# A Fourier-mixing kernel on one core: channel mixing added straight from PSUM, a fourth y buffer, and another order of waiting work

## The chip, the cores and the metric

One Trainium2 chip, one of its cores. Five engines run their own instruction streams in order and meet through semaphores: TensorE (PE, with its weight loads shown as PEld), VectorE (DVE), ScalarE (ACT), GpSimd (POOL) and SyncE (SP), which here issues every DMA. The metric is the device time of one execution in microseconds.

## The reference

Eight batches of 3136 tokens with 256 channels. A global filter in the frequency domain (along the tokens), then a mixing block: real part of a two-dimensional FFT, a residual, a layer norm and two dense layers.

```python
X = np.fft.rfft(x, axis=1)
Y = X * (filt_r + 1j * filt_i)[None, :, :]
x = np.fft.irfft(Y, n=x.shape[1], axis=1)

mixed = np.real(np.fft.fft(np.fft.fft(x, axis=1), axis=2))
u = x + mixed
un = (u - mean(u)) / np.sqrt(var(u) + 1e-06)
out = u + np.maximum(un @ w_ch1, 0.0) @ w_ch2
```

w_ch1 is 256 by 1024, w_ch2 1024 by 256.

## The kernel before

All FFTs are matrix products on PE, with float32 operands split into two float16 parts (a high part, cast by ACT, and the remainder, subtracted by DVE or POOL); three products hh, hl, lh give the accuracy. The FFT of 3136 = 112 x 28 is done in two stages each way, with a DMA through DRAM between the stages to turn the layout.

Per batch b these steps run as generators that the main loop advances a step at a time:

- forward1: seven loads x (L319), a maximum over each for scaling (mx, absmax, L257), then 14 times: cast and subtract (x16), three matmuls into bank s1 (L343), copy and remainder (ast), and a store to d1 (L347).
- forward2: seven loads at from d1 (L367); spectrum: matmuls into bank s2 (L388, L389), product with the filter on DVE and POOL (yt, t2), split and transpose by DMA into z (L414); fold: sums eo, which the channel mixing reads later; inverse1: matmuls (L450 to L452), split into bt, store to d2 (L456).
- inverse2: seven loads b2 from d2 (L484), 14 times matmuls into bank y (L502), scaling by ACT into ys (L509), and stores to dy in DRAM (L488). dy is the filtered x.

The second part works on groups of 256 frequency slots, that is two tiles t of 128, each with both tokens k of a slot (which share the mixed spectrum); there are 49 groups. fetch(g) loads y from dy (L558) into one of three buffers. prepare(g) does the channel mixing on PE into a PSUM bank pm (mix, L571), lets ACT copy it scaled to m (L619), lets POOL form sums and differences sd of the two halves (both, L581 and L582), lets DVE add them to y (add, L588 and L589), computes the layer norm's statistics (st, mv, sb: L639 to L656), the normalized un on DVE (L663), its split u16 (ACT L668, then POOL L670), and transposes it by DMA into ut (L671). Then come eight pairs of products per group: first_product into bank h (L693), ReLU by ACT (L702) and remainder by DVE (L703); second_product into acc (L722), two pairs later; after the eighth, DVE adds acc to y (L731) and y is stored (L734). A product below is one of these 392 pairs.

PSUM has eight banks: four named psf, which s1, s2, i1, y, mix and some small ones share in turn, two for h, two for acc.

The order has two makers. The main loop (L893) emits products and, between them, steps of the FFT stages of coming batches, paced by constants (RISE, EARLY, SOON, LOAD_AT and so on). A scheduler then lays out each engine's instructions in an order of its own, in which ready work can pass work that waits; after(key) forbids that: what is emitted under it stands behind the marked instruction. On the chip every engine, SP's DMA queue too, takes its list strictly in order.

Of the kernel before, what the change touches and what calls it, by code (L numbers as in the profile page):

```python
# [35 lines left out]
STEPS = 22 + 7 * 5  # L36
BACK = 14
EARLY = 0.4
RISE = 30
SOON = 860  # L40
LOAD_AT = (15, 16, 17, 18, 19, 25, 26, 23)
LOAD_AFTER = (6, 7, 8, 9, 10, None, None, None)
LOAD_IN = ("ys", "ys", "ys", "ut", "ut", "ys", "ys", "ys")
WIDEN_AT = (22, 22, 26, 50, 51, 52, 53, 53)
BOUND_AT = (60, 73)
SPLIT_AT = (60, 98)
# [143 lines left out]
def _program(ctx, tc, nc, a, NB):  # L190
# [33 lines left out]
    ones = cp.tile([1, 128], F32, name="ones")  # L224
    eo = cp.tile([128, 2, 2, RING], F16, name="eo")
# [7 lines left out]
    nc.vector.memset(ones, 1.0)  # L233
    nc.scalar.activation(beta[:1], ones[:, 0:1], AF.Sqrt)
# [121 lines left out]
    def forward2(b, d1, d2):  # L356
        al = cp.tile([128, 2], F32, name=f"alpha_{b}")
        nc.vector.tensor_tensor(al[:, 0:1], sxs[b][:, 0:1], pF[:, 0:1], op=ALU.mult)
        nc.vector.tensor_scalar(al[:, 1:2], al[:, 0:1], 1.0 / 64, None, op0=ALU.mult)
# [17 lines left out]
        def spectrum(ch, hf):  # L377
# [5 lines left out]
            p = bank(f"s2_{b}_{ch}_{hf}")[:, :448].rearrange("p (r n) -> p r n", r=2)  # L383
            for u in range(8):
# [3 lines left out]
                nc.tensor.matmul(o, w, s2[:, U, 0].rearrange("p (r k) -> p r k", r=2), start=True, stop=False)  # L388
# [72 lines left out]
        far = 2 if b else 3  # L461
        for c in range(far):
            load(c)
        for c in range(9):
# [9 lines left out]
    def inverse2(b, d2):  # L474
# [6 lines left out]
        def load(c):  # L481
            if c < 7:
                bts[c] = fp.tile([112, 4, 2, 256], F16, tag="b2", name=f"b2_{b}_{c}", bufs=2)
                nc.sync.dma_start(bts[c].rearrange("p j h c -> p (j h) c"), d2v[:, 8 * c : 8 * c + 8])  # L484

        def store(k, s, r, ys, c, j0):
            rows = dy[k, 224 * c : 224 * c + 224].rearrange("(j s q) c -> s q j c", j=4, s=2)
            nc.sync.dma_start(rows[s, :, j0], ys[r : r + 28, j0])  # L488

        load(0)  # L490
        for c in range(14):
# [7 lines left out]
            for js, t in parts:  # L499
                for i in range(2):  # L500
                    for h in range(2):
                        nc.tensor.matmul(  # L502
                            p[64 * h : 64 * h + 64, js],
                            i2[:, t, h, i],
                            bt[:, o + js.start : o + js.stop, h],
                            start=i == 0,
                            stop=i == 1,
                        )
            nc.scalar.activation(ys[:, o : o + 2], p, AF.Copy, scale=al[:, 1:2])  # L509
# [69 lines left out]
    def both(sd, m):  # L579

        nc.gpsimd.tensor_tensor(sd[..., 0, :], m[..., 1:128], m[..., 129:], op=ALU.add)  # L581
        nc.gpsimd.tensor_tensor(sd[..., 1, :], m[..., 1:128], m[..., 129:], op=ALU.subtract)  # L582

    def add(o, mm, parts):

        for h in range(2):
            c = slice(128 * h + 1, 128 * h + 128)
            nc.vector.tensor_tensor(o[..., c], o[..., c], parts[h], op=ALU.add)  # L588
# [375 lines left out]
```

## Time and profile before

| | us |
|---|---|
| median of 3 runs | 1606.58 (1602.94 to 1613.36) |
| profiled execution | 1607.78, span 1605.9 |
| granted TensorE clock, mean | 0.946 |
| DMA moved | 273 MB, mean 170 GB/s |
| ACT, POOL instructions | 1302, 803 |

The profile shows one execution. The page's first part gives an engine's busy time and its share of the span; a window row the same for a stretch of it, with the granted clock and the share of the time in which the 16 DMA engines were busy. A waits row says which instruction stood idle for whom, in total, how often and how long at most. A group row has the instructions of one line and shape: count, busy time, mean of one, and the idle time of their engine just ahead of them. A timeline row has its start, its length, and in brackets the idle time before it with what ended that.

The start has its own character: in the first 160 us the clock granted to TensorE was 0.66 on average, and products began at 159.

### The profile page before, as it was taken

What the parts mean: (1) busy time and instruction counts of PE and PEld (TensorE: products, weight loads), DVE (VectorE), ACT (ScalarE), POOL (GpSimd) and SP (SyncE); (2) the same over time, 40 slices, a digit from 0 to 9 for tenths busy, and PEclk for the clock granted to TensorE, in tenths of its full rate; (3) what the DMA queues carried; (4) which work ended last, traced back from release to release, by engine and by line L of the source; (5) the groups of instructions that cost most, each with busy time, mean ns of one, the idle gap of its engine ahead of it and who ended that gap; (6) DMA issues with size and microseconds to landing.
All of it is one profiled execution on the core that took longest, in us unless ns stands there. A gap on an engine that the chain in (4) does not pass through costs nothing. (4 is left out here: it accounts for less than half of the span.)

```text
span 1605.9 us, 30431 instructions
## 1 busy us (share of the span) xinstructions
PE 1414.0 (88%) x11217; PEld 943.0 (59%) x11217; DVE 1142.5 (71%) x2557; ACT 706.2 (44%) x1302; POOL 634.4 (40%) x803
## 2 busy tenths in 40 slices
PE   4344989898989989898988999899998999999998
PEld 1332666566665656555665666556675666666666
DVE  7784978697676668686667877767877779655552
ACT  4454634363435444363433643345543645433331
POOL 4463058216722176114751165311861057421110
PEclk9555999999999999999999999999999999999999
DMA  7999558867875786756875786855987488634430
GB/s 232 262 204 246 132 139 179 207 173 178 183 193 146 185 178 152 214 152 156 195 176 157 196 176 153 206 152 158 208 187 189 133 208 195 160 100 125 114 78 27
DMA packets 446261, 273.14 MB, mean 170 GB/s; under 512 B 235392, under 2 KB 412592, under 8 KB 446112
## 3 DMA queue, kind: packets, MB, share of 16 engines
q1 hardware_dynamic: 446112, 271.20, 68.6%
q8 instruction: 88, 1.44, 0.4%
q14 instruction: 61, 0.50, 0.1%
HBM read 113.31 MB, written 102.76 MB: 135 GB/s over the span
## 5 line engine op out<-in xcount | busy, mean ns | idle before, releaser
L693 PE MATMUL h<-ut,w1s 128*128 128x512 f16 x2352 | 593.6, 387 | 40.9 <-DVE h L703 37.9
L722 PE MATMUL acc<-w2s,h 128*128 128x256 f16 x4704 | 595.8, 275 | 17.3 <-DVE y L731 15.6
L722 PEld LDWEIGHTS <-h 128*128 128x128 f16 x4704 | 458.8, 99 | 151.3 <-issue 30.1
L703 DVE SCALAR_TENSOR_TENSOR h<-h,h 128x512 f16<-128x512 f32 x392 | 266.9, 683 | 215.2 <-ACT h L702 214.6
L702 ACT ACTIVATE h<-h 128x512 f16<-128x512 f32 x392 | 232.4, 596 | 386.7 <-PE h L693 378.2
L693 PEld LDWEIGHTS <-w1s 128*128 128x128 f16 x2352 | 224.5, 99 | 273.2 <-issue 82.8
L670 POOL TENSOR_TENSOR u<-un,u 128x512 f16<-128x512 f32 x94 | 110.9, 1194 | 370.9 <-ACT u L668 276.2
L581 POOL TENSOR_TENSOR sd<-m 128x254 f32<-128x254 f32 (+1 forms) x64 | 41.9, 655 | 317.8 <-ACT m L619 278.6
L401 POOL TENSOR_TENSOR yt<-yt,t 128x224 f32<-128x224 f32 x105 | 70.4, 671 | 151.7 <-DVE t L397 90.8
L588 DVE TENSOR_TENSOR y<-y,sd 128x254 f32<-128x254 f32 (+1 forms) x224 | 104.7, 511 | 23.3 <-DMA y<-dy 22.8
L409 POOL TENSOR_TENSOR y<-yt,y 128x448 f16<-128x448 f32 x105 | 110.7, 1058 | 14.0 <-ACT y L405 13.7
L343 PE MATMUL s<-x,s 112*112 112x512 f16 x336 | 100.7, 403 | 7.5 <-DVE x L338 5.4
L509 ACT ACTIVATE ys<-y,alpha 128x512 f32<-128x512 f32 x112 | 76.4, 688 | 66.1 <-PE y L502 56.1
L405 ACT CAST y<-yt 128x448 f16<-128x448 f32 x112 | 62.9, 564 | 85.6 <-POOL yt L402 83.8
L388 PE MATMUL s<-s,at 112*128 112x56 f16 x896 | 67.1, 194 | 35.6 <-DMA at<-d 27.0
L257 DVE TENSOR_REDUCE mx<-x 112x1 f32<-112x1024 f32 x56 | 67.8, 1213 | 40.5 <-DMA x<-x 40.4
L502 PE MATMUL y<-b,i 112*64 112x512 f16 (+1 forms) x480 | 76.8, 403 | 21.6 <-DMA b<-d 21.2
L455 DVE TENSOR_TENSOR bt<-i,bt 112x512 f16<-112x512 f32 x112 | 75.2, 680 | 26.1 <-ACT bt L454 26.0
L393 DVE TENSOR_TENSOR yt<-s,ft 128x448 f32<-128x448 f32 x112 | 68.2, 613 | 35.5 <-PE s L389 34.8
L454 ACT CAST bt<-i 112x512 f16<-112x512 f32 x112 | 64.9, 582 | 62.8 <-PE i L452 39.8
L345 ACT CAST ast<-s 112x512 f16<-112x512 f32 x112 | 65.2, 583 | 61.4 <-PE s L343 52.2
L338 DVE SCALAR_TENSOR_TENSOR x<-x,sx,x 112x512 f16<-112x512 f32 x111 | 89.2, 808 | 2.8 <-ACT x L337 2.3
(130 smaller groups left out, 1826.7 us busy)
## 6 DMA issues: line engine op xcount, KB each, us to landing
x<-x SPq DMA_DIRECT2D x56, 448.0 KB
d<-ast SPq DMA_DIRECT2D x112, 224.0 KB
at<-d SPq DMA_DIRECT2D x56, 448.0 KB
d<-bt SPq DMA_DIRECT2D x112, 224.0 KB
b<-d SPq DMA_DIRECT2D x56, 448.0 KB
out<-y SPq DMA_DIRECT2D x98, 256.0 KB
y<-dy SPq DMA_DIRECT2D x92, 256.0 KB
dy<-ys SPq DMA_DIRECT2D x208, 112.0 KB
```

The costliest lines, as they stand in the source:

```text
L338: nc.vector.scalar_tensor_tensor(x16[:, 1], x, sx[:112, 1:2], x16[:, 0], op0=ALU.mult, op1=ALU.subtract)
L343: marks["pe", q] = nc.tensor.matmul(p, s1[:, hs], x16[:, hx], start=i == 0, stop=i == 2).ins
L409: last = half(b, hf == 1).tensor_tensor(y16[:, :, 1, :112], ytv, y16[:, :, 0, :112], op=ALU.subtract)
L455: nc.vector.tensor_tensor(bt[:, :, 1], p, bt[:, :, 0], op=ALU.subtract)
L502: nc.tensor.matmul(p[64 * h : 64 * h + 64, js], i2[:, t, h, i], bt[:, o + js.start : o + js.stop, h], start=i == 0, stop=i == 1,)
L509: nc.scalar.activation(ys[:, o : o + 2], p, AF.Copy, scale=al[:, 1:2])
L588: nc.vector.tensor_tensor(o[..., c], o[..., c], parts[h], op=ALU.add)
L670: marks["u16", g] = low.tensor_tensor(u16[:m, :, :, 1], unv, u16[:m, :, :, 0], op=ALU.subtract).ins
L693: nc.tensor.matmul(p[:, c0 : c0 + n].rearrange("p (t k q) -> p t k q", k=2, q=m), w1s[:, d, hw, 128 * f : 128 * f + 128], utv[:, ts, :, d, ...
L702: nc.scalar.activation(h[:, 0, :nt], p[:, :nt], AF.Relu)
L703: nc.vector.scalar_tensor_tensor(h[:, 1, :nt], p[:, :nt], 0.0, h[:, 0, :nt], op0=ALU.max, op1=ALU.subtract)
L722: nc.tensor.matmul(acc[:m, k], h[:, hh, c0 : c0 + m], w2s[:, f, hw], start=f == 0 and k == 0 and i == 0, stop=f == 7 and k == 1 and i == 2,)
```

## The change

- DVE now adds the mixed channels to y straight from the PSUM bank pm, scaled by alpha or its negative in the same instruction: per tile one addition over 4 x 127 elements, two over 2 x 127, one over the four end channels. The copies m and the sums sd, with their tiles, are gone; a single row's Nyquist part is added by itself (add_nyquist).
- un is computed by ACT (scale and bias) instead of DVE; the steps for sb are written as fewer fused operations, and EPS is ACT's bias.
- y has four buffers instead of three. fetch(g + 2) is called two products earlier, and its load stands behind the output of the group four back.
- The maxima over x run two loads behind their loads and stand behind an h of the products; the adds to y stand behind an h; the first s2 matmul and the first y matmul of a batch stand behind a first product; loads of b2 stand behind the latest store to dy.
- forward2 keeps three loads at ahead for every batch, takes two empty steps (PAUSE) after them, and inverse2 one; the pacing constants are set anew. Of these numbers the diff shows only some.

```diff
-BACK = 14
-EARLY = 0.4
-RISE = 30
-SOON = 860
+PAUSE = 2
+BACK = 15
+EARLY = 0.5
+RISE = 28
+SOON = 930
...
     def forward1(b, d1):
...
-        for q in range(7):
+        lag = 2 if b else 0
+        for q in range(7 + lag):
             with after(("y", 0), ("un", 0)) if b == 1 else nullcontext():
-                nc.sync.dma_start(xs[q], a["x"][b, :, 4 * q : 4 * q + 4])
-                absmax(m[:, q : q + 1], xs[q], AX.XY)
-            yield
+                if q < 7:
+                    nc.sync.dma_start(xs[q], a["x"][b, :, 4 * q : 4 * q + 4])
+                if q >= lag:
+                    with after("h"):
+                        absmax(m[:, q - lag : q - lag + 1], xs[q - lag], AX.XY)
+            if q < 7:
+                yield
...
+            order = after("pe") if b and ch == 0 else nullcontext()
...
+                with order if u == 0 else nullcontext():
+                    nc.tensor.matmul(o, w, s2[:, U, 0].rearrange("p (r k) -> p r k", r=2), start=True, stop=False)
...
-        far = 2 if b else 3
+        far = 3
         for c in range(far):
             load(c)
+        for _ in range(PAUSE):
+            yield
...
-                nc.sync.dma_start(bts[c].rearrange("p j h c -> p (j h) c"), d2v[:, 8 * c : 8 * c + 8])
+                with after("dy"):
+                    nc.sync.dma_start(bts[c].rearrange("p j h c -> p (j h) c"), d2v[:, 8 * c : 8 * c + 8])
...
-        y = ys_of[g] = mp.tile([128, 2, 2, 256], F32, tag="y", name=f"y_{g}", bufs=3)
+        y = ys_of[g] = mp.tile([128, 2, 2, 256], F32, tag="y", name=f"y_{g}", bufs=4)
...
-                with after(("ut", 0)) if g == 2 else nullcontext():
+                with after(("ut", 0)) if g == 2 else after(("out", g - 4)):
...
+    def scaled_add(out, p, al, y):
+
+        nc.vector.scalar_tensor_tensor(out, p, al, y, op0=ALU.mult, op1=ALU.add)
+
+    def add(o, pm, al):
+
+        n = o.shape[0]
+        oh = o.rearrange("p k (h c) -> p (k h) c", h=2)
+        even = pm[:, 1:128].unsqueeze(1).to_broadcast([n, 4, 127])
+        odd = pm[:, 129:].unsqueeze(1).to_broadcast([n, 2, 127])
+        ends = pm[:, 0:129:128].unsqueeze(1).to_broadcast([n, 2, 2])
+        scaled_add(oh[..., 1:], even, al[:, 0:1], oh[..., 1:])
+        for hs, sign in ((slice(0, 4, 3), 0), (slice(1, 3), 1)):
+            scaled_add(oh[:, hs, 1:], odd, al[:, sign : sign + 1], oh[:, hs, 1:])
+        scaled_add(o[..., 0:129:128], ends, al[:, 0:1], o[..., 0:129:128])
...
-        for ps, ts, al in runs:
-            nc.scalar.activation(m[ps, ts], pm[ps, ts], AF.Copy, scale=al)
-            both(sd[ps, ts], m[ps, ts])
-        yield
-        for k in range(2):
-            for ps, ts, al in runs:
-                with after(("u16", 0)) if g == 1 else nullcontext():
-                    add(y[ps, ts, k], m[ps, ts], (sd[ps, ts, k], sd[ps, ts, 1 - k]))
...
+        for t, (g0, g1) in enumerate(tiles):
+            ps = slice(0, g1 - g0)
+            with after(("u16", 0)) if g == 1 else after("h"):
+                add(y[ps, t], pm[ps, t], alpha_of(g0, g1, f"al_{g}_{t}")[ps])
...
-            nc.vector.tensor_scalar(v, v, EPS, None, op0=ALU.add)
-            nc.scalar.activation(r, v, AF.Sqrt)
+            nc.scalar.activation(sb[:m, ks, 0], mv[:m, ks, 1], AF.Sqrt, bias=eps[:m])
...
-                marks["un", g] = nc.vector.tensor_scalar(
-                    un[:m, k], y[:m, t, k], mv[:m, i, 0:1], sb[:m, i, 2:3], op0=ALU.subtract, op1=ALU.mult
-                ).ins
+                nc.scalar.activation(un[:m, k], y[:m, t, k], AF.Identity, bias=sb[:m, i, 1:2], scale=sb[:m, i, 3:4])
...
-        if f == 2 and g + 2 < ng:
+        if f == 0 and g + 2 < ng:
             bring(groups[g + 2][-1][1] - 1)
             fetch(g + 2)
```

How the built program's instructions stand in three places. In the names the first number is the batch or the group, the next the step; h16_9_5 is h of group 9, fifth pair counted from 0. First DVE, where the maxima of batch 3 (mx_3) meet the products of group 9. Before:

```order
L703 SCALAR_TENSOR_TENSOR h16_9_4_5390<-h_9_4_5383,h16_9_4_5390 128x512
L257 TENSOR_REDUCE mx_3_5557<-x_3_0_5550 112x1
L455 TENSOR_TENSOR bt_2_5_1_5423<-i1_2_5_1_5416,bt_2_5_1_5423 112x2x256
L257 TENSOR_REDUCE mx_3_5557<-x_3_1_5551 112x1
L703 SCALAR_TENSOR_TENSOR h16_9_5_5434<-h_9_5_5427,h16_9_5_5434 128x512
L589 TENSOR_TENSOR y_11_5340<-y_11_5340,m_11_5394 128x2x2 x2
L257 TENSOR_REDUCE mx_3_5557<-x_3_2_5552 112x1
L588 TENSOR_TENSOR y_11_5340<-y_11_5340,sd_11_5395 128x2x127 x4
L257 TENSOR_REDUCE mx_3_5557<-x_3_3_5553 112x1
L455 TENSOR_TENSOR bt_2_6_0_5464<-i1_2_6_0_5457,bt_2_6_0_5464 112x2x256
L257 TENSOR_REDUCE mx_3_5557<-x_3_4_5554 112x1
L703 SCALAR_TENSOR_TENSOR h16_9_6_5475<-h_9_6_5468,h16_9_6_5475 128x512
```

The same engine and place after:

```order
L715 SCALAR_TENSOR_TENSOR h16_9_3_5373<-h_9_3_5366,h16_9_3_5373 128x512
L260 TENSOR_REDUCE mx_3_5364<-x_3_0_5357 112x1
L715 SCALAR_TENSOR_TENSOR h16_9_4_5398<-h_9_4_5391,h16_9_4_5398 128x512
L260 TENSOR_REDUCE mx_3_5364<-x_3_1_5358 112x1
L715 SCALAR_TENSOR_TENSOR h16_9_5_5444<-h_9_5_5437,h16_9_5_5444 128x512
L260 TENSOR_REDUCE mx_3_5364<-x_3_2_5359 112x1
L715 SCALAR_TENSOR_TENSOR h16_9_6_5476<-h_9_6_5469,h16_9_6_5476 128x512
L597 SCALAR_TENSOR_TENSOR y_11_5274<-mix_11_5401,alpha_1_1858,y_11_5274 128x4x127
L260 TENSOR_REDUCE mx_3_5364<-x_3_3_5360 112x1
L597 SCALAR_TENSOR_TENSOR y_11_5274<-mix_11_5401,alpha_1_1858,y_11_5274 128x2x127 x2
L597 SCALAR_TENSOR_TENSOR y_11_5274<-mix_11_5401,alpha_1_1858,y_11_5274 128x4
L597 SCALAR_TENSOR_TENSOR y_11_5274<-mix_11_5401,alpha_1_1858,y_11_5274 128x4x127
```

Between two h there stood up to three maxima, and in these rows now one. Second SP's queue shortly before, where the loads of y_11 and x_3 and the output of group 8 stand. Before:

```order
L734 DMA out<-y_8_4077 128x2x256 x2
L671 DMA_TRANSPOSE ut_10_5189<-u16_10_0_5300 128x8x128
L456 DMA d2_2_3099<-bt_2_4_0_5325 112x1024
L558 DMA y_11_5340<-dy_1_3057 128x2x256
L456 DMA d2_2_3099<-bt_2_4_1_5336 112x1024
L414 DMA_TRANSPOSE z_2_6_5177<-y16_1_103 128x8x128
L558 DMA y_11_5340<-dy_1_3057 128x2x256
L671 DMA_TRANSPOSE ut_10_5189<-u16_10_1_5356 128x8x128
L319 DMA x_3_0_5550<-x 112x1024
```

The same queue and place after:

```order
L324 DMA x_3_4_5361<-x 112x1024
L467 DMA d2_2_3029<-bt_2_4_1_5175 112x1024
L574 DMA y_11_5274<-dy_1_2981 128x2x256 x2
L324 DMA x_3_5_5362<-x 112x1024
L467 DMA d2_2_3029<-bt_2_5_0_5221 112x1024
L467 DMA d2_2_3029<-bt_2_5_1_5232 112x1024
L467 DMA d2_2_3029<-bt_2_6_0_5270 112x1024
L324 DMA x_3_6_5363<-x 112x1024
L746 DMA out<-y_8_4046 128x2x256 x2
```

The load of y_11 stood behind the output of group 8 and ahead of the loads x_3; now it stands behind the first five of those loads and ahead of that output. Third DVE where group 5 is made ready (its adds to y_5). Before:

```order
L703 SCALAR_TENSOR_TENSOR h16_3_5_3012<-h_3_5_3005,h16_3_5_3012 128x512
L455 TENSOR_TENSOR bt_1_5_0_2990<-i1_1_5_0_2983,bt_1_5_0_2990 112x2x256
L455 TENSOR_TENSOR bt_1_5_1_3001<-i1_1_5_1_2994,bt_1_5_1_3001 112x2x256
L589 TENSOR_TENSOR y_5_2896<-y_5_2896,m_5_2961 128x2x2 x2
L703 SCALAR_TENSOR_TENSOR h16_3_6_3080<-h_3_6_3073,h16_3_6_3080 128x512
L588 TENSOR_TENSOR y_5_2896<-y_5_2896,sd_5_2962 128x2x127 x4
L639 BN_STATS st_5_3166<-y_5_2896 128x6 x4
```

The same engine and work after:

```order
L715 SCALAR_TENSOR_TENSOR h16_4_7_3524<-h_4_7_3517,h16_4_7_3524 128x512
L597 SCALAR_TENSOR_TENSOR y_5_2820<-mix_5_3007,alpha_0_393,y_5_2820 128x4x127
L245 TENSOR_REDUCE row_x2_3162<-pt_x2_3160 1x1
L597 SCALAR_TENSOR_TENSOR y_5_2820<-mix_5_3007,alpha_0_393,y_5_2820 128x2x127 x2
L597 SCALAR_TENSOR_TENSOR y_5_2820<-mix_5_3007,alpha_0_393,y_5_2820 128x4
L597 SCALAR_TENSOR_TENSOR y_5_2820<-mix_5_3007,alpha_0_393,y_5_2820 128x4x127
```

The adds to y_5 stood behind the sixth and seventh h of group 3, ten products ahead of group 5's first; now they stand behind the last h of group 4.

More of the change, by code (lines that the diff above doesn't have):

```diff
@@ L224, in _program @@
     ones = cp.tile([1, 128], F32, name="ones")
+    eps = cp.tile([128, 1], F32, name="eps")
     eo = cp.tile([128, 2, 2, RING], F16, name="eo")
@@ L356, in forward2 @@
     def forward2(b, d1, d2):
[L357 removed]
+        al = cp.tile([128, 3], F32, name=f"alpha_{b}")
         nc.vector.tensor_tensor(al[:, 0:1], sxs[b][:, 0:1], pF[:, 0:1], op=ALU.mult)
[L359 removed]
+        nc.vector.tensor_scalar(al[:, 1:2], al[:, 0:1], -1.0, None, op0=ALU.mult)
+        nc.vector.tensor_scalar(al[:, 2:3], al[:, 0:1], 1.0 / 64, None, op0=ALU.mult)
         alphas[b] = al
@@ L498, in inverse2 @@
             parts = [(slice(0, 1), 0), (slice(1, 2), 1)] if c == 0 else [(slice(0, 2), 1)]
[L499 to L509, printed above, removed]
+            with after("pe") if c == 0 else nullcontext():
+                for js, t in parts:
+                    for i in range(2):
+                        for h in range(2):
+                            nc.tensor.matmul(
+                                p[64 * h : 64 * h + 64, js],
+                                i2[:, t, h, i],
+                                bt[:, o + js.start : o + js.stop, h],
+                                start=i == 0,
+                                stop=i == 1,
+                            )
+            nc.scalar.activation(ys[:, o : o + 2], p, AF.Copy, scale=al[:, 2:3])
             if o:
@@ L609, in prepare @@
             yield
-        same = len({g0 // NS for g0, _ in tiles} | {(g1 - 1) // NS for _, g1 in tiles}) == 1
-        if same and len(tiles) == 2 and all(g1 - g0 == 128 for g0, g1 in tiles):
-            runs = [(slice(0, 128), slice(0, 2), alphas[tiles[0][0] // NS][:, 0:1])]
-        else:
-            runs = [
-                (slice(0, g1 - g0), slice(t, t + 1), alpha_of(g0, g1, f"al_{g}_{t}")[: g1 - g0])
-                for t, (g0, g1) in enumerate(tiles)
-            ]
-        for ps, ts, al in runs:
-            nc.scalar.activation(m[ps, ts], pm[ps, ts], AF.Copy, scale=al)
-            both(sd[ps, ts], m[ps, ts])
-        yield
-        for k in range(2):
-            for ps, ts, al in runs:
-                with after(("u16", 0)) if g == 1 else nullcontext():
-                    add(y[ps, ts, k], m[ps, ts], (sd[ps, ts, k], sd[ps, ts, 1 - k]))
-            if k == 0:
-                for t, s, pn, al in fix:
-                    nc.scalar.activation(m[s, t], pn, AF.Copy, scale=al[s, 0:1])
-                    both(sd[s, t], m[s, t])
+        for t, s, _, _ in fix:
+            keep = mp.tile([128, 2, 256], F32, tag="un", name=f"keep_{g}", bufs=2)[:, 0]
+            nc.scalar.copy(keep[s], y[s, t, 1])
+        for t, (g0, g1) in enumerate(tiles):
+            ps = slice(0, g1 - g0)
+            with after(("u16", 0)) if g == 1 else after("h"):
+                add(y[ps, t], pm[ps, t], alpha_of(g0, g1, f"al_{g}_{t}")[ps])
+        for t, s, pn, al in fix:
+            add_nyquist(y[s, t, 1], pn, al[s], keep[s])
         yield
@@ L775, in widen_weights @@
             if i % 2 == 0:
-                pairs[0] = mp.tile([128, 2, 512], F32, tag="y", name=f"w_{i}", bufs=3)
+                pairs[0] = mp.tile([128, 2, 512], F32, tag="y", name=f"w_{i}", bufs=4)
             w = pairs[0][:, i % 2]
```

63 lines of the change are left out of this document (30 added, 33 removed).

## The prediction

> **What bounds the kernel now.** I read the busy shares first, then four windows of the trace, the waits inside the long one, and last the timeline at single waits. One page line and the windows (columns: stretch, its length, then busy us and count of PE, PEld, DVE, ACT, POOL, then clock, DMA share, GB/s):
> ```profile
> PE 1414.0 (88%) x11217; PEld 943.0 (59%) x11217; DVE 1142.5 (71%) x2557; ACT 706.2 (44%) x1302; POOL 634.4 (40%) x803
> ...
> 0.00:160.00 160.00, 67.94 (x473) 45.27 (x474) 111.61 (x216) 80.12 (x158) 76.85 (x91) 0.66 0.89 236
> 160.00:350.00 190.00, 174.07 (x1338) 114.67 (x1337) 154.90 (x346) 92.78 (x171) 73.91 (x97) 0.95 0.70 170
> 350.00:1410.00 1060.00, 981.50 (x8045) 658.30 (x8044) 773.99 (x1740) 472.87 (x866) 456.66 (x583) 0.98 0.72 175
> 1410.00:1605.90 195.90, 190.51 (x1365) 124.79 (x1363) 101.97 (x258) 60.37 (x108) 26.97 (x32) 1.00 0.36 88
> ```
> TensorE bounds the kernel from 160 us on, and the change removes none of its matmuls. So all that can be won is its idle time: 92 us in the first stretch, 16, 78.5 and 5 in the others. The first 160 us belong to the DMA queues (share 0.89). The 78.5 us are told by the waits of PE in that window (us, times, longest):
> ```profile
> PE h L693 <- DVE h L703: 32.0, 30, 2.7
> PE s L388 <- DMA at<-d: 16.1, 13, 3.4
> PE acc L722 <- DVE y L731: 11.3, 15, 2.6
> PE y L502 <- DMA b<-d: 9.0, 4, 4.6
> PE i L450 <- DVE mx L257: 2.5, 1, 2.5
> ```
> Two rows of DVE make 43.3 us, two rows of loads 25.1. Why DVE is late shows in its timeline, below with the PE rows that follow from it:
> ```profile
> 458.57 0.68 DVE L703 SCALAR_TENSOR_TENSOR h<-h,h 128x512 f16<-128x512 f32 x1
> 466.15 1.22 DVE L257 TENSOR_REDUCE mx<-x 112x1 f32<-112x1024 f32 x1 [6.90 <-DMA x<-x]
> 467.29 0.68 DVE L455 TENSOR_TENSOR bt<-i,bt 112x512 f16<-112x512 f32 x1
> 467.88 1.21 DVE L257 TENSOR_REDUCE mx<-x 112x1 f32<-112x1024 f32 x1
> 469.01 0.68 DVE L703 SCALAR_TENSOR_TENSOR h<-h,h 128x512 f16<-128x512 f32 x1
> ...
> 469.74 2.64 PE L693 MATMUL h<-ut,w1s 128*128 128x512 f16 x6 [2.67 <-DVE h L703]
> 476.19 1.46 PE L693 MATMUL h<-ut,w1s 128*128 128x512 f16 x6 [1.56 <-DVE h L703]
> ```
> DVE takes its instructions in order. A maximum over x stood ahead of the products' h and waited 6.90 us for x; PE then stood 2.67, 1.56 and more while DVE worked off what had piled up. The other two causes are adds to y that wait for y, and runs of un ahead of the sums that free an accumulator. DVE's own waits for transfers in the same window, then such a run and the PE wait behind it:
> ```profile
> DVE y L589 <- DMA y<-dy: 38.9, 17, 4.8
> DVE mx L257 <- DMA x<-x: 25.5, 9, 6.9
> DVE y L588 <- DMA y<-dy: 8.9, 2, 6.2
> ...
> 577.32 2.46 DVE L663 TENSOR_SCALAR un<-y,mv,sb 128x256 f32<-128x256 f32 x4
> 579.70 0.74 DVE L731 SCALAR_TENSOR_TENSOR y<-acc,beta,y 128x512 f32<-128x512 f32 x1
> ...
> 580.49 1.44 PE L722 MATMUL acc<-w2s,h 128*128 128x256 f16 x6 [2.60 <-DVE y L731]
> ```
>
> **The change part by part.** The group rows that price it (count, then busy us, mean ns of one):
> ```profile
> L588 DVE TENSOR_TENSOR y<-y,sd 128x254 f32<-128x254 f32 x168 | 88.2, 574 | 11.4 <-DMA y<-dy 11.3
> L588 DVE TENSOR_TENSOR y<-y,sd 128x127 f32<-128x127 f32 x56 | 16.5, 322 | 11.9 <-DMA y<-dy 11.5 <-POOL sd L581 0.4
> L589 DVE TENSOR_TENSOR y<-y,m 128x4 f32<-128x4 f32 x84 | 32.1, 418 | 35.6 <-DMA y<-dy 25.8 <-ACT bt L454 4.4 <-ACT h L702 3.5
> L589 DVE TENSOR_TENSOR y<-y,m 128x2 f32<-128x2 f32 x28 | 6.1, 237 | 21.4 <-DMA y<-dy 13.2 <-ACT m L619 8.3
> L731 DVE SCALAR_TENSOR_TENSOR y<-acc,beta,y 128x512 f32<-128x512 f32 x98 | 71.1, 742 | 12.0 <-PE acc L722 12.0
> L393 DVE TENSOR_TENSOR yt<-s,ft 128x448 f32<-128x448 f32 x112 | 68.2, 613 | 35.5 <-PE s L389 34.8 <-POOL ef L422 0.4
> L257 DVE TENSOR_REDUCE mx<-x 112x1 f32<-112x1024 f32 x56 | 67.8, 1213 | 40.5 <-DMA x<-x 40.4
> L663 DVE TENSOR_SCALAR un<-y,mv,sb 128x256 f32<-128x256 f32 x196 | 78.1, 457 | 1.3
> L653 DVE TENSOR_TENSOR sb<-sb 128x4 f32<-128x4 f32 x49 | 13.8, 282 | 1.2
> L619 ACT ACTIVATE m<-mix,alpha 128x512 f32<-128x512 f32 x42 | 28.8, 685 | 13.9 <-PE mix L571 12.9 <-POOL yt L401 0.7 <-DVE y L589 0.4
> L619 ACT ACTIVATE m<-mix,alpha 128x256 f32<-128x256 f32 x8 | 3.7, 473 | 0.9 <-PE mix L571 0.9
> ```
> Added from PSUM: out go DVE's L588 and L589, 88.2 + 16.5 + 32.1 + 6.1 = 142.9 us, ACT's copies (28.8 + 3.7) and POOL's sums and differences. In come four scaled adds for each of 98 tiles, of 508, 254, 254 and 4 elements, one operand in PSUM. The nearest row is L731, the same operation at 512 elements: 742 ns. For smaller ones I take the slope between L393 (448, 613 ns) and L257 (1024, 1213 ns), 1.04 ns an element: 738, 474, 474 and 214, together 1.90 us. Neighbours overlap: of the rows above, the one at 466.15 lasts 1.22 us and the next starts at 467.29, 0.08 before its end, so four less 0.08 each, 1.58 us, is the lower end. That is 155 to 186 us on DVE, 12 to 43 more than goes out. The mean of L588 holds slowed pieces too, so I lean to the upper half, +30.
>
> un moves to ACT: DVE loses 78.1 us; ACT gains 196 times 473 ns (L619 at that size) = 93 and loses its copies of 33. From 706 busy us that makes 766, 48% of the span; the run of un now stands in ACT's queue ahead of the products' h instead of DVE's. Of the small steps for sb six become five: one of 49 times 282 ns less, -14. DVE in all: 1142.5 + 30 - 78 - 14 = 1080, between 1062 and 1093. None of that is on the path by itself, since PE sets the end; it counts where DVE is behind.
>
> Held behind the products: the maxima run two loads behind their transfer and each behind an h already issued; the adds to y stand behind an h as well, and y is fetched two steps earlier into a fourth buffer. Before, a fetch waited for the output of the group three back:
> ```profile
> SPq L558 <- DMA out<-y: 55.2, 25, 5.0
> ```
> With four buffers that output has long landed, so SP no longer stands there, with ut and d queued behind it; a late dy store can still hold a fetch. The order shown above for batch 3 does as the text says: h stand between the maxima, and y 11 is loaded ahead of the output of group 8. So the causes of 43.3 + 2.5 us go. I take three quarters, 34 us: where the maxima, the adds and the x of the next batch meet, DVE still has about as much to do between two h as PE: the wait at 476.19 above came ten us after x had. Ends: a third (15) if that load keeps PE standing, all (46).
>
> Loads (the matmuls of at and of b): the first of each batch is held behind products on PE. Between the last s1 and the first s2 of a batch, and between the last inverse matmul and the first y, the order has about as much product work as before (some 9 us for both), so the transfer itself is no better covered; what helps is the freer SP queue. Of 25.1 us I take 7; ends -5 (the pacing moved against me) and 18.
>
> Start: first products stand behind a PE wait for the maxima of batch 1,
> ```profile
> 159.03 0.34 PE L240 MATMUL pt_x<-ident,mx 112*1 112x112 f32 x1 [12.94 <-DVE mx L322]
> ```
> and in the changed order they come ahead of those maxima. ut's own transposes are issued only shortly before, so of 12.94 I take 5 (0 to 10). What is moved out comes back: batch 1's forward step now starts at product 10 instead of 2, DVE is fuller from there to product 48, and group 5 starts late (the third order place; group 3 is nearly as close): its adds stand behind the last h of group 4, ten products later than before, so that the chain from add to transpose lies between two groups with little else for PE. I estimate some 8 us for it, in a stretch which already lost 16; with the waits that vanish there it cancels, 0 (-10 to +8).
>
> A bank of PSUM is now held until y has come, not until ACT has copied. The order puts the bank's next user one to three products behind the add nearly everywhere, so I cost it at 1 us; if the cover is gone PE waits for the bank in place of h. The other pacing numbers move work by a few products and cost nothing while PE has products to do.
>
> Sum, against the profiled execution (1607.8 us with 1605.9 of span, 1.2 above the median of the runs): 34 + 7 + 5 + 0 - 1 = 45, so 1562.8; against the median 1562.
>
> **The skill against it.** The Trainium skill, "VectorE: DVE Perf Modes", section "Rules for kernel authors", says of elementwise work on a matmul's output to accept the slower rate or to copy to SBUF first if many operations follow. Four per tile are many, and this change does the reverse. The rows agree in direction, 12 to 43 us more on DVE; they do not show DVE to be the bound, at 71%.
>
> **Rivals.** (a) The waits only move: DVE is as late as before since its load per group hardly falls (62 us in 1142), and PE waits for the late h all the same, or for at and b. For it: DVE at 773.99 of 1060 us is uneven, with back-to-back stretches as behind 469. Against: the waits begin at transfers that are told apart by name. Then only a third of DVE's 46 us and the start are won: 1608 - 15 - 3 = 1590, between 1585 and 1608.
> (b) Slower: groups start late. The add is tied behind an h, mixing behind a bank, and the chain add, statistics, un, transposes gets longer than the products ahead of it cover, as at group 5. Each later group would then make PE wait at its first product. With 47 groups it cancels the gain of 45 at 0.96 us a group, and at 1.4 us gives 1607 - 45 + 66 = 1628. For it: the third order place. Against: at group 11 the last adds stand nine products ahead of their group, and of the 49 groups only 0, 3 and 5 have fewer than five.
> (c) Slower by the adds: all 43 us of the upper price ahead of h, with the waits for loads as before and nothing won: 1650. It decides where DVE's work between two h passes PE's. The un that leave (78 us) speak against it. This is what the Trainium skill's rule above comes to, taken to its end.
> (d) All of the DVE waits, the upper ends of loads and start: 46 + 18 + 10 = 74, so 1533.
>
> **How the numbers follow.** Forecast 1562, its own range 1537 to 1590: chance 0.62. (a) 0.20, (b) 0.10, (c) 0.03, (d) 0.05. A measurement of this kernel can tell about 1% from no change, that is 1590 and 1623. Under 1590 lie the forecast, (d) and a third of (a): 0.73. Over 1623 most of (b) and (c): 0.10. The rest, 0.17, is within 1%. The range that leaves out no more than 0.2 goes from the low end of the forecast to the high end of (a), 1537 to 1606.
>
> **What would show it.** Right: in the middle stretch PE's waits for DVE h and y together fall from 43 to about 10 us, DVE's waits for x and y nearly vanish, PE's idle time there falls from 78 to below 45; the new adds have means near 740, 470 and 210 ns; DVE's busy time falls by about 60 us, ACT's rises by 55; waits for at and b stay at 15 to 20 us. Wrong: a wait of h for ut at the start of most groups (rival b), PE waiting for a bank behind the adds, or ACT's un as the releaser of h. The first products should start before 159 us.

## The result, and the profile after

Before: 1609.97 us median (1602.94 to 1615.50, 4 runs). After: 1569.85 us (1563.13 to 1572.55, 4 runs), a ratio of 0.9759 with a 95% interval of 0.9725 to 0.9792: 40 us less, where 1562 was forecast. The profiled execution of the changed kernel took 1570.7 us, with a span of 1568.9. Busy times of the whole span, from its page:

```profile
PE 1403.9 (89%) x11217; PEld 939.2 (60%) x11217; DVE 1092.5 (70%) x2409; ACT 773.6 (49%) x1442; POOL 541.1 (34%) x675
```

DVE fell by 50 us, POOL by 93, ACT rose by 67. To see where the time went, both kernels are cut at the same work, not at the same time: at the start of the products number 0, 48 and 328 (number 8g + f is the f-th of group g). The windows of before (stretch, length, busy us and count of PE, PEld, DVE, ACT, POOL, clock, DMA share, GB/s):

```profile
0.00:159.30 159.30, 67.24 (x472) 45.00 (x473) 111.10 (x213) 80.12 (x158) 76.85 (x91) 0.66 0.89 236
159.30:353.50 194.20, 178.27 (x1364) 116.91 (x1363) 158.91 (x358) 93.75 (x172) 73.91 (x97) 0.95 0.69 169
353.50:1417.30 1063.80, 985.30 (x8071) 660.70 (x8069) 775.51 (x1744) 474.40 (x869) 458.60 (x588) 0.98 0.72 175
1417.30:1605.90 188.60, 183.22 (x1318) 120.41 (x1316) 96.96 (x243) 57.87 (x103) 25.04 (x28) 1.00 0.35 87
```

And those of after:

```profile
0.00:160.90 160.90, 66.64 (x450) 44.23 (x451) 109.02 (x228) 81.09 (x160) 71.49 (x85) 0.63 0.90 231
160.90:367.60 206.70, 182.50 (x1399) 119.27 (x1399) 153.61 (x325) 103.66 (x191) 63.50 (x81) 0.94 0.67 165
367.60:1382.00 1014.40, 972.14 (x8052) 655.24 (x8053) 735.78 (x1630) 520.57 (x966) 390.23 (x495) 0.98 0.78 183
1382.00:1568.90 186.90, 182.58 (x1320) 120.46 (x1317) 94.06 (x229) 68.24 (x125) 15.90 (x14) 1.00 0.36 86
```

The first 160 us lost 1.6, the first 48 products lost 12.5, the middle won 49.4 and the end 1.7: 37.0 of span. In the middle TensorE's idle time fell from 78.5 to 42.3 us, and its busy time by 13.2 for 19 matmuls less, more than those cost; the modelled ends of matmuls take in waits too short to be listed, and how much of the 13.2 is that was not told apart. TensorE's waits in the middle stretch of after (us, times, longest):

```profile
PE y L518 <- DMA b<-d: 21.7, 5, 7.4
PE s L399 <- DMA at<-d: 14.1, 8, 4.4
PE h L705 <- DMA ut<-u: 3.9, 4, 2.1
PE acc L734 <- DVE y L743: 2.8, 4, 1.2
PE h L705 <- DVE h L715: 1.4, 2, 0.8
```

The waits for DVE are nearly gone: 45.8 us (h 32.0, y 11.3, mx 2.5) became 4.2. Those for the loads of at and b grew from 25.1 to 35.8, those for ut from 1.3 to 3.9. DVE's own waits for transfers from 350 to 1375 us, and SP's waits ahead of the loads of y over the whole span:

```profile
DVE y L597 <- DMA y<-dy: 2.2, 3, 1.2
...
SPq L574 <- DMA out<-y: 20.7, 10, 3.9
SPq L574 <- DMA dy<-ys: 67.6, 63, 4.1
```

Before, DVE waited 47.8 us for y and 25.5 for x (350 to 1410 us), and SP 55.2 for outputs. But SP stood at the same loads for the stores of dy too, and that row was

```profile
SPq L558 <- DMA dy<-ys: 32.3, 38, 4.2
```

So SP's two waits ahead of the loads of y make 88.3 us now and made 87.5 before: with four buffers it waits for dy instead of the outputs. In the stretch of the first 48 products these waits of TensorE are new or grew (z stood at 1.6 us before):

```profile
PE h L705 <- DMA ut<-u: 11.3, 4, 6.4
PE i L461 <- DMA z<-y: 7.4, 2, 6.6
PE pb_x L256 <- DVE mv L655: 3.1, 1, 3.1
```

Of the 11.3 us for ut, 6.4 end with the first product and so lie in the stretch ahead; 2.1 end with product 48 and are in the 3.9 above as well.

The groups of the moved work, by shape (count, then busy us, mean ns of one):

```profile
L597 DVE SCALAR_TENSOR_TENSOR y<-mix,alpha,y 128x254 f32<-128x254 f32 x184 | 79.3, 471 | 1.0
L597 DVE SCALAR_TENSOR_TENSOR y<-mix,alpha,y 128x508 f32<-128x508 f32 x92 | 67.8, 737 | 13.8 <-PE mix L587 6.6 <-ACT keep L638 4.4 <-DMA y<-dy 2.9
L597 DVE SCALAR_TENSOR_TENSOR y<-mix,alpha,y 128x4 f32<-128x4 f32 x92 | 19.6, 213 | 0.0
L677 ACT ACTIVATE un<-y,sb 128x256 f32<-128x256 f32 x196 | 101.8, 590 | 30.6 <-DVE sb L670 30.5
```

### The profile page after: what moved, and what is told of

It is laid out like the page before. It is cut to its first block, busy times and chain, and to the rows that moved or that the text cites. A ratio compares the mean times of both kernels' runs of the same rounds, so it can differ in the third digit from the quotient of the medians.

```text
span 1568.9 us, 30185 instructions
## 1 busy us (share of the span) xinstructions
PE 1403.9 (89%) x11217; PEld 939.2 (60%) x11217; DVE 1092.5 (70%) x2409; ACT 773.6 (49%) x1442; POOL 541.1 (34%) x675
## 4 chain that ended last, share of the span: by engine, by line
PE 59%; DMA 16%; DVE 10%; issue 6%; POOL 4%; ACT 4%; SPq 1%; DVEq 0%; ACTq 0%; POOLq 0%
PE h L705 24%; PE acc L734 22%; PE y L518 3%; PE s L351 3%; DMA b<-d 3%; DMA at<-d 3%; DMA d<-bt 2%; DMA d<-ast 2%; PE mix L587 2%; DVE y L597 2%; DMA ut<-u 2%; PE i L461 1%; DMA x<-x 1%; DMA z<-y 1%; PE s L399 1%
## 5 line engine op out<-in xcount | busy, mean ns | idle before, releaser
L705 PE MATMUL h<-ut,w1s 128*128 128x512 f16 x2352 | 589.9, 385 | 16.6 <-DMA ut<-u 13.1
L597 DVE SCALAR_TENSOR_TENSOR y<-mix,alpha,y 128x508 f32<-128x508 f32 (+1 forms) x368 | 156.0, 473 | 14.8 <-PE mix L587 6.6
L677 ACT ACTIVATE un<-y,sb 128x256 f32<-128x256 f32 x196 | 101.8, 590 | 30.6 <-DVE sb L670 30.5
L518 PE MATMUL y<-b,i 112*64 112x512 f16 (+1 forms) x480 | 77.7, 413 | 41.9 <-DMA b<-d 41.8
L351 PE MATMUL s<-x,s 112*112 112x512 f16 x336 | 105.5, 412 | 8.1 <-DVE x L346 5.3
L399 PE MATMUL s<-s,at 112*128 112x56 f16 x896 | 67.1, 194 | 32.5 <-DMA at<-d 25.3
L354 DVE TENSOR_TENSOR ast<-s,ast 112x512 f16<-112x512 f32 x112 | 75.8, 680 | 24.9 <-ACT ast L353 24.7
L461 PE MATMUL i<-z,i 112*112 112x256 f16 x224 | 66.2, 295 | 26.7 <-DMA z<-y 18.3
```

Of the source, the lines that this page charges most:

```text
L351: marks["pe", q] = nc.tensor.matmul(p, s1[:, hs], x16[:, hx], start=i == 0, stop=i == 2).ins
L518: nc.tensor.matmul(p[64 * h : 64 * h + 64, js], i2[:, t, h, i], bt[:, o + js.start : o + js.stop, h], start=i == 0, stop=i == 1,)
L597: nc.vector.scalar_tensor_tensor(out, p, al, y, op0=ALU.mult, op1=ALU.add)
L677: nc.scalar.activation(un[:m, k], y[:m, t, k], AF.Identity, bias=sb[:m, i, 1:2], scale=sb[:m, i, 3:4])
L705: marks["pe"] = nc.tensor.matmul(p[:, c0 : c0 + n].rearrange("p (t k q) -> p t k q", k=2, q=m), w1s[:, d, hw, 128 * f : 128 * f + 128], ut ...
```

## The experiments

All are the changed kernel with one edit, unless said otherwise; each is timed against the kernel before on the same chip. The question of the first four: which part of the change took DVE's waits away?

**Maxima not held** (e_max). Each maximum over x stands behind its own load again.

```diff
-        lag = 2 if b else 0
+        lag = 0
...
-                    with after("h"):
+                    with nullcontext():
```

> The changed kernel with the maxima over x as in the kernel before: each right behind its own load, none held behind an h. Theory (each hold removes the DVE wait it stands at): DVE's waits for x come back in the middle stretch (25 us before, none in the changed kernel), and TensorE's waits for DVE's h with them, by the share of x in DVE's waits before, 25.5 of 73.3 of the 39 us gained: 13 us slower than the changed kernel, about 1583; ends 7 and 20. Rival (what won the time is the freer queue of SP and the fourth buffer of y; the maxima wait but are covered): DVE's waits for x come back and the time stays within 4 us of 1570.

Neither: 1537.36 us (1530.03 to 1539.71), ratio 0.9552 (0.9522 to 0.9582), 33 us faster than the changed kernel. Its two stretches up to product 328:

```profile
161.40:357.90 196.50, 179.92 (x1386) 117.67 (x1386) 147.11 (x328) 103.73 (x192) 63.45 (x81) 0.95 0.71 173
357.90:1348.90 991.00, 964.30 (x8064) 653.68 (x8065) 732.52 (x1636) 521.96 (x966) 390.85 (x495) 0.99 0.79 188
```

TensorE's waits in the second of them, and DVE's for x there:

```profile
PE h L705 <- DVE h L715: 10.2, 7, 4.7
PE y L518 <- DMA b<-d: 6.1, 4, 3.3
PE s L399 <- DMA at<-d: 5.0, 4, 2.3
PE acc L734 <- DVE y L743: 2.7, 2, 1.7
...
DVE mx L260 <- DMA x<-x: 22.6, 14, 4.8
```

The theory's mechanism is there (DVE waits 22.6 us for x, TensorE 8.8 more for h) and is outweighed: the waits for loads fall from 35.8 to 11.1, and the stretch of the first 48 products is 10 us shorter. What the hold delays shows at batch 3, in rows of SP, DVE and PE: the last load of x, the last maximum, the first matmul of s1. The changed kernel:

```profile
461.43 0.32 SPq L324 DMA_DIRECT2D x<-x  x1
486.90 2.33 DVE L260 TENSOR_REDUCE mx<-x 112x1 f32<-112x1024 f32 x2
503.19 0.38 PE L351 MATMUL s<-x,s 112*112 112x512 f16 x1
```

Without the hold:

```profile
455.60 0.43 SPq L324 DMA_DIRECT2D x<-x  x1
461.75 1.19 DVE L260 TENSOR_REDUCE mx<-x 112x1 f32<-112x1024 f32 x1
483.44 2.11 PE L351 MATMUL s<-x,s 112*112 112x512 f16 x9
```

From the last load's issue to the last maximum's end is 27.8 us with the hold and 7.3 without, and to the first matmul of s1 41.8 and 27.8: s1 comes 14 us later against its load. In the built orders the first s1 of batches 3 to 7 stands two to six products later with the hold, while the first matmul on b stands at the same product or one earlier. Between the last inverse matmul and that first matmul on b, batches 2 to 5 then have 9.1, 9.1, 8.5 and 8.4 us of products, and 10.4, 12.3, 13.0 and 12.3 without the hold. With the hold taken away and the lag kept, every engine's order is the same as here: without the hold the lag does nothing.

The long window, below, is that from 350 to 1375 us. **Adds not held** (e_add), y as in the changed kernel:

```diff
-            with after(("u16", 0)) if g == 1 else after("h"):
+            with after(("u16", 0)) if g == 1 else nullcontext():
```

> The changed kernel with the adds to y no longer held behind an h; four buffers and the early load of y stay. Theory (the two measures for y do the same thing twice: y has landed before the adds are due, since it is fetched two products earlier and behind an output that is long gone): DVE's waits for y stay below 8 us, the time stays within 4 us of 1570. Rival (the hold is what keeps the adds off the transfer): DVE's waits for y rise above 20 us and the time to 1580 or more.

1572.95 us, ratio 0.9785 (0.9764 to 0.9806): no difference from the changed kernel (0.9759, the intervals overlap). **y in three buffers, loaded as before** (e_y3), the hold kept:

```diff
-        y = ys_of[g] = mp.tile([128, 2, 2, 256], F32, tag="y", name=f"y_{g}", bufs=4)
+        y = ys_of[g] = mp.tile([128, 2, 2, 256], F32, tag="y", name=f"y_{g}", bufs=3)
...
-                with after(("ut", 0)) if g == 2 else after(("out", g - 4)):
+                with after(("ut", 0)) if g == 2 else nullcontext():
...
-        if f == 0 and g + 2 < ng:
+        if f == 2 and g + 2 < ng:
```

> The changed kernel with y in three buffers and loaded at the third product of a group as before; the holds stay. Theory: the adds stand behind an h but their y comes as late as before, SP waits some 50 us again for outputs that have to land before a load of y, and DVE's waits for y come back to 20 us or more: 1582, 12 us slower, with ends 5 and 25. Rival (the hold alone takes the adds past the landing of y): SP's wait comes back, DVE's does not, and the time stays within 4 us of 1570.

1570.20 us, ratio 0.9758 (0.9731 to 0.9786), no difference; the rival holds. DVE's waits for y in the long window without the hold, then with three buffers, and there SP's wait for outputs:

```profile
DVE y L597 <- DMA y<-dy: 6.8, 5, 2.6
```

```profile
DVE y L597 <- DMA y<-dy: 5.1, 3, 2.0
...
SPq L574 <- DMA out<-y: 63.9, 23, 6.6
```

SP stands for outputs again, and nobody is late for it. With either measure alone the 47.8 us of before stay away; whether they come back with both away, or the rest of the change keeps them off too, was not tried.

**un on DVE** (e_un): one line at L677.

```diff
-                nc.scalar.activation(un[:m, k], y[:m, t, k], AF.Identity, bias=sb[:m, i, 1:2], scale=sb[:m, i, 3:4])
+                nc.vector.tensor_scalar(
+                    un[:m, k], y[:m, t, k], sb[:m, i, 3:4], sb[:m, i, 1:2], op0=ALU.mult, op1=ALU.add
+                )
```

> The changed kernel with un on DVE as before (bias and scale as the changed kernel works them out). Theory: DVE's busy time rises by about 80 us to 1172, ACT's falls by about 100 to 672, and the runs of un stand ahead of the sums that free an accumulator again: TensorE's wait for y at the second product, 2.8 us in the middle stretch of the changed kernel, returns to about 11, that for h rises by some us; 1580, 10 us slower. In the first 160 us it may gain 2 to 4, since u16 of group 0 then no longer waits for ACT. Rival (DVE has the time, 1092 busy of 1569): within 4 us of 1570.

1587.02 us, ratio 0.9867 (0.9848 to 0.9887): 17 us slower, more than expected. The first products begin at 158.4 us instead of 160.9; the middle (products 48 to 328) takes 1031.6 instead of 1014.4. TensorE's waits for DVE's y and h there are 6.9 us, hardly above 4.2; so the named path carries only a small part of it. Its waits for transfers there rise more, from 40.0 to 49.0 (ut 3.9 to 8.3, z 0.3 to 3.7, at 14.1 to 15.5). Why those come later was not settled.

**Mixed channels copied to SBUF** (e_copy): ACT copies, POOL sums, DVE adds from SBUF, as before the change. The copies' buffers leave room for three y only, so it is compared with e_y3.

```diff
+            nc.scalar.activation(m[ps, ts], pm[ps, ts], AF.Copy, scale=al)
+            both(sd[ps, ts], m[ps, ts])
...
-                add(y[ps, t], pm[ps, t], alpha_of(g0, g1, f"al_{g}_{t}")[ps])
+                    add_parts(y[ps, ts, k], m[ps, ts], (sd[ps, ts, k], sd[ps, ts, 1 - k]))
```

> The changed kernel with y in three buffers (that alone ran at 1570, as the changed kernel) and the mixed channels copied to SBUF by ACT, summed by POOL and added from SBUF by DVE as before; everything else of the change stays. Theory: POOL's busy time rises by about 93 us to 635 and ACT's by 33 to 806, DVE's falls by about 13; the sums stand in POOL's queue between the spectra's work and lengthen the way from mixing to the adds: 1580, ends 1572 and 1592. Rival (those engines have the time; adds from PSUM win nothing): within 4 us of 1570.

1589.78 us, ratio 0.9890 (0.9851 to 0.9929) against 0.9758 for e_y3: 21 us slower. Busy times of e_y3, then of e_copy:

```profile
PE 1408.8 (90%) x11217; PEld 941.1 (60%) x11217; DVE 1105.1 (70%) x2409; ACT 773.2 (49%) x1442; POOL 542.4 (34%) x675
```

```profile
PE 1413.8 (89%) x11217; PEld 939.6 (59%) x11217; DVE 1061.5 (67%) x2353; ACT 798.6 (50%) x1498; POOL 624.2 (39%) x787
```

The copy takes 44 us from DVE and still costs 21: DVE is then busy for less and late more often (TensorE waits 12.3 us for its h in the long window, 1.4 in e_y3). The 44 is a high figure, since DVE is busier in e_y3 than in any other run of the same instructions (1087 to 1095); against the changed kernel's 1092.5 it is 31. Why DVE is late with less to do is likely what the section on the hardware shows: its adds from SBUF stand still beside POOL's work.

**Why does the hold cost?** e_early keeps it and starts each batch's forward step earlier:

```diff
-EARLY = 0.5
+EARLY = 0.6
```

> The changed kernel, holds and lag kept, with EARLY 0.6 in place of 0.5: a batch's forward step, its loads of x included, starts some five products earlier. Theory (the hold of the maxima costs time because the scale of x, and with it the first s1, comes three to five products later while the last inverse matmul stays where it is, so the stores and loads between lie closer to their use): in the order the first s1 of batches 3 to 7 now stand at products 80 to 278, as without the hold (82 to 278), so TensorE's waits for at and b in the middle stretch fall from 36 to below 18 us and the time to about 1548, ends 1535 and 1558, and DVE still doesn't wait for x. Rival (the hold costs by itself: x stays in its buffers longer, and the maxima stand in front of other work of DVE): 1565 to 1575 as the changed kernel.

1572.67 us, ratio 0.9788 (0.9753 to 0.9824): the rival. TensorE's longest waits in the long window:

```profile
PE s L399 <- DMA at<-d: 25.3, 7, 7.3
PE h L705 <- DMA ut<-u: 8.8, 5, 3.6
PE i L461 <- DMA z<-y: 4.8, 6, 1.5
```

The waits for b vanished (in batches 2 to 6 the order now leaves 20 us and more of products between the last inverse matmul and the first on b), and those for at grew from 14.1 to 25.3. But here the long window begins 28 us ahead of product 48. Cut at the products, at is 20.4 in the middle, which takes 1007.9 us instead of 1014.4, and the first 48 products take 217.1 instead of 206.7: what the earlier start won in the middle was lost ahead of it. An earlier start does not give back what the hold takes; why at comes later was not settled. **One more step ahead of b** (e_b16) asks whether cover decides:

```diff
-BACK = 15
+BACK = 16
...
         load(0)
         yield
+        yield
```

> The changed kernel with one more empty step between the first load of b and the first product that reads it (16 steps of the inverse instead of 15). In the order the product work between a batch's last inverse matmul and the first matmul on its b grows from 9.1 to 15.6 and 16.9 us in batches 2 and 3 and stays at 8.2 to 9.1 in batches 4 to 7; between the last s1 and the first s2 it hardly changes. Theory (a load makes TensorE wait where the order leaves it less product work than store, load and queue take, some 12 to 18 us from last inverse matmul to first use): the waits for b of batches 2 and 3, 2.2 and 7.4 us in the changed kernel, vanish, those of 4 to 6, 12 us, stay; the time falls by 8 us to 1562, ends 1556 and 1567. Rival (SP's queue or the DMA engines' load makes them, so that moving the use moves the wait): the sum for b stays near 21 us, or goes over to at, and the time stays within 4 us of 1570.

1560.61 us, ratio 0.9704 (0.9674 to 0.9735), 9 us below the changed kernel; the two intervals just overlap (its 0.9735 against the other's 0.9725). The theory, batch by batch: the waits of batches 2 and 3 (2.15 and 7.39 us in the changed kernel) are gone, those of 4 to 6 stay.

```profile
PE y L519 <- DMA b<-d: 11.3, 4, 4.1
PE h L706 <- DMA ut<-u: 9.8, 7, 6.3
PE s L399 <- DMA at<-d: 5.4, 7, 2.5
```

The waits for at fell too, by 8.7 us, though the order gives them little more cover; that was not foreseen. **Hold and pacing, crossed.** e_maxpace has the pacing of before and no hold on the maxima, e_pace the pacing of before and the hold:

```diff
-PAUSE = 2
-BACK = 15
-EARLY = 0.5
-RISE = 28
-SOON = 930
+PAUSE = 0
+BACK = 14
+EARLY = 0.4
+RISE = 30
+SOON = 860
...
-                with after("dy"):
+                with nullcontext():
```

With these go the empty step behind the first load of b, the ties of a batch's first matmuls behind the products, the third early load of at, and the slots of the weights' loads.

> The changed kernel without hold and lag on the maxima (that ran at 1537), and all pacing as in the kernel before: no pause, 14 steps of the inverse, EARLY, RISE, SOON, loads of b not behind the dy stores. What is left of the change is un on ACT, the adds from PSUM held behind h, four buffers of y. Theory (these shorten DVE's and POOL's work, and that won the time; pacing only mends what the hold shifts): within 8 us of 1537, up to 1545. Rival (pacing carries most of what the kernel without the hold gains over the kernel before): 1570 or more, with TensorE's waits for at and b in the middle stretch at 25 us or more, against 11 without the hold and 25 in the kernel before.

> The changed kernel with hold and lag on the maxima kept and all pacing as in the kernel before (the same without the hold ran at 1564). Theory (the hold costs at any pacing: it puts some ten more us between the last x and the first s1 of a batch, and the loads of at and b lose that much cover): 20 us slower than 1564, about 1584, ends 1574 and 1600, with 25 us or more of TensorE's waits for at and b in the middle stretch, 15 us or less for DVE. Rival (the hold is bad only with the new pacing, which starts the inverse's products earlier): within 6 us of 1564, or faster.

1563.69 us, ratio 0.9728 (0.9702 to 0.9754), and 1593.21 us, 0.9897 (0.9866 to 0.9928). The four corners: without the hold 0.9552 (new pacing) and 0.9728 (old), with it 0.9759 and 0.9897. Their differences, of 1607 us: the hold costs 33 us in the new pacing and 27 in the old, and the new pacing wins 28 without the hold and 22 with it. So the hold costs in both pacings, as the theory of e_pace had it. In the profiles the new pacing, without the hold, wins 39 us in the middle (1030.4 to 991.1) and loses 12 in the first 48 products (184.9 to 196.5). For e_maxpace both sides missed the time: 26 us above 1537, with 28.5 us of waits for at and b in the long window as the rival said, but 44 below the kernel before.

**Neither hold** (e_hold): the edits of e_max and e_add together.

> The changed kernel with neither hold: maxima right behind their loads, adds to y not held behind an h; four buffers and the early load of y stay. Without the hold on the maxima alone it ran at 1537, without that on the adds alone at 1573. Theory (the hold on the adds wins nothing, since y has landed): DVE's waits for y below 8 us and the time within 6 us of 1537. The order leaves 8.3 to 10.9 us of product work ahead of b in batches 2 to 6 here, against 8.3 to 13.0 with the adds held, so the upper half, near 1541, is likelier. Rival (with the maxima free, the hold on the adds is what keeps DVE ahead of the products): TensorE's waits for DVE's h rise from 10 to above 18 us, the time to 1550 or more.

1538.08 us, ratio 0.9565 (0.9524 to 0.9605): as e_max. The hold on the adds wins nothing there either.

**Faster than both.** Two on top of e_max: RISE 32 instead of 28 (e_maxrise), and that with the edit of e_b16 and un of group 0 alone on DVE (e_best).

```diff
-RISE = 28
+RISE = 32
...
-                nc.scalar.activation(un[:m, k], y[:m, t, k], AF.Identity, bias=sb[:m, i, 1:2], scale=sb[:m, i, 3:4])
+                if g == 0:
+                    nc.vector.tensor_scalar(
+                        un[:m, k], y[:m, t, k], sb[:m, i, 3:4], sb[:m, i, 1:2], op0=ALU.mult, op1=ALU.add
+                    )
+                else:
+                    nc.scalar.activation(
+                        un[:m, k], y[:m, t, k], AF.Identity, bias=sb[:m, i, 1:2], scale=sb[:m, i, 3:4]
+                    )
```

> The changed kernel without hold and lag on the maxima (1537), and RISE 32 in place of 28: batch 1's steps come slower among the first products. Theory (in the start stretch groups 3 and 5 begin late because batch 1 is pressed into too few products; now the adds of group 3 stand 9 products ahead of it instead of 7, of group 5 10 instead of 1): product 48 starts 4 to 8 us earlier than the 357.9 there, and the time falls to 1531, ends 1526 and 1536. Rival (those products wait for transfers of batch 1 that only come later now): no change or up to 6 us slower.

> The changed kernel without hold and lag on the maxima, RISE 32 (these two together ran at 1534), 16 steps of the inverse, and un of group 0 alone on DVE. Theory (un of group 0 waits for nothing on DVE, as where all un were on DVE and the first products began at 158.4 instead of 161; cover for b of batches 2 to 4 grows from 10.4, 12.3 and 13.0 to 15.6, 18.7 and 13.0 us): the first products begin near 159, TensorE's waits for b fall from 6.7 to about 4 us, and the time to 1528, ends 1521 and 1534. Rival (what is won in the start stretch waits for batch 1 again, and a later use of b presses the inverse's other steps): 1534 to 1540.

1533.62 us, ratio 0.9541 (0.9515 to 0.9567), and 1531.27 us, 0.9519 (0.9478 to 0.9560). Neither is told from e_max's 0.9552. In e_maxrise product 48 begins 10 us earlier (347.5 against 357.9) and product 56 only 1.3 (390.8 against 392.1). TensorE's waits between the two are 6.6 us against 4.4, but its matmul instructions 364 against 310: the slower pace moved work behind product 48 more than it won time. In e_best the first product begins at 163.4, not near 159, so what delays ut of group 0 is not un on ACT alone. By the ratios these two run 74 and 77 us below the kernel before (of 1607) and 35 and 39 below the changed one.

## Why the prediction was right, and where it was not

The time was within 8 us, and the mechanism named as what could be won (TensorE's waits for a late DVE) was what went. But the terms missed by more than their sum, and that the sum came so near is in part luck: loads, start and batch 1 came out 37 us worse than taken, the DVE waits 8 better, and 13 us of TensorE's busy time in the middle, which no term held, went too.

- **DVE waits, +34.** They went nearly whole: 45.8 to 4.2, +41.6. The step "So the causes of 43.3 + 2.5 us go" had the right size and the wrong agent. The hold on the maxima, which was to do it, keeps TensorE from 8.7 us of DVE waits (12.9 without, 4.2 with it); the hold on the adds and the fourth buffer, each taken away alone, change nothing. With that hold away and the old pacing (e_maxpace) h and y are at 21.1: about half of the 45.8 went with the new adds, un and the measures for y.
- **un and the adds, "None of that is on the path by itself".** This step failed. Undone, un costs 17 us and the adds from PSUM 21, and with the hold away and the old pacing the rest of the change (un, the adds, the steps for sb, the measures for y) wins 44. So most of the gain is here. That it comes by DVE being less late for h shows for the adds (1.4 us of waits for h against 12.3); for un it shows only in part (6.9 us of waits for h and y against 4.2), and the waits for transfers grew more.
- **"The other pacing numbers move work by a few products and cost nothing".** This step failed too: the pacing as a whole, with the ties of a batch's first matmuls and the third early load of at, is worth 22 to 28 us.
- **Loads, +7 (-5 to +18).** Measured 10.7 us worse, 13.3 with ut, outside the range. The step was "so the transfer itself is no better covered; what helps is the freer SP queue". At the loads of y SP was not freer (87.5 to 88.3): what it no longer waits for outputs it waits for dy, which the prediction had seen as possible ("a late dy store can still hold a fetch") and not priced. Nor was the cover of b "about as much": in the built orders batches 2 to 4 had 11.7, 10.1 and 10.0 us of products ahead of it and have 9.1, 9.1 and 8.5. The hold makes the forward step start later with its end where it was: e_max took 25 us of these waits away.
- **Start, +5 (0 to +10).** The first products began 1.6 us later. They no longer wait for the maxima of batch 1, but 6.42 us for ut: in ACT's rows, weights and y copies stand between un at 142.02 and the cast of u at 148.05. "ut's own transposes are issued only shortly before" was seen and cost too little.
- **Batch 1 later, 0 (-10 to +8).** The stretch lost 12.5 us, 8.3 of it idle time. Without the hold it lost 2.3, and in the old pacing it took 202.7 us with the hold and 184.9 without: most of the loss is the hold's.
- **Sizes.** Scaled adds 737, 471, 213 ns where 738, 474, 214 were taken; DVE 1092.5 where 1062 to 1093 was given; un on ACT 590 ns where 473 was taken from a pass of the same size out of PSUM, so ACT stands at 774, not 766. The bank of PSUM: TensorE waited for none.
- **Rivals.** (a) came in a part that it named: waits moved to at and b, 10.7 us of them, but DVE's went whole, not by a third. (b) came at seven products of the whole span (13.1 us for ut, 1.3 before), not at most groups; (c) and (d) did not come. The rule of the Trainium skill, "VectorE: DVE Perf Modes", section "Rules for kernel authors", to copy to SBUF first if many operations follow, would have spoken for e_copy. The trace agrees that the copy relieves DVE, by 31 to 44 us, but the time is 21 us worse.

Each taken away alone, the parts close only roughly: 17 + 21 + (22 to 28) - 33 makes 27 to 33 of 40 us. Put in one after the other they close, as they must: un, adds and what goes with them 44 (e_maxpace), new pacing 28 (e_max), hold -33, together 39. Inside the 44, what un and the adds (17 + 21) leave was not told apart.

## What to carry to other kernels

A wait that an in-order engine takes for a transfer is cheap while the bound engine has work queued; tying the waiting operation behind that work frees the engine, but delays all that depends on its result (here at a cost of 27 to 33 us), and that chain is to be followed to its end before the tie is made. When several edits come at once, an engine "off the path" is still worth relieving if its lateness, not its share, is what the bound engine waits for, at once or through the transfers that it feeds. A queue is freer only if all its waits together fall. Cut two traces at the same work, not the same time, before comparing stretches.

## What the runs showed of the hardware

DVE's adds with both operands in SBUF had a long tail, those with one in PSUM none. From the two kernels' answers for the old lines and the new one (minimum, median, maximum ns):

```profile
L588 DVE TENSOR_TENSOR y<-y,sd x224: 247/412/2242, 135.9 to 1550.1; 128x254 f32<-128x254 f32 x84, 128x127 f32<-128x127 f32 x28
```

```profile
L597 DVE SCALAR_TENSOR_TENSOR y<-mix,alpha,y x368: 203/471/748, 133.9 to 1522.3; 128x508 f32<-128x508 f32 x92, 128x254 f32<-128x254 f32 x92
```

```profile
L589 DVE TENSOR_TENSOR y<-y,m x112: 130/164/4395, 136.6 to 1550.4; 128x4 f32<-128x4 f32 x84, 128x2 f32<-128x2 f32 x28
```

The mean of the old 254-element add (574 ns) was above that of the new one (471) though its typical piece was not. The Trainium skill, "SBUF — State Buffer", section "🔬 SBUF: two separate sides", says that a DVE operation with two SBUF inputs and a GpSimd operation that reads SBUF take a shared pair of ports by an exclusive lock. This trace fits that: of the 336 old adds, 101 took over 1.3 times the median of their size, and every one of the 101 overlapped an operation on POOL; no add that overlapped none took over 1.05 times its median. Of the 392 new ones 133 overlapped POOL and none was slow, and in e_copy all 70 slow adds again overlapped it. The longest, two adds of four elements in one row:

```profile
246.61 4.47 DVE L589 TENSOR_TENSOR y<-y,m 128x4 f32<-128x4 f32 x2 [0.36 <-ACT m L619]
```

POOL's operations stand without a gap from 246.60 to 250.98, and DVE's next h starts at 251.00. Over their medians the slow adds cost the old kernel 53 us of DVE's time. How much of the 40 us that is was not told apart. On ACT, un with scale and bias from SBUF took 590 ns for 256 elements, as long as a cast of 512 from PSUM (583).
